# Attention into a bilinear FFN on one core: g turned ahead of the first x, K chunks reordered in the first two units, last half group copied by one engine

## The chip, the cores and the metric

The kernel runs on one core of a Trainium2 chip. The metric is the device time of one launch in microseconds (us). Each time is the median of several runs. "Span" is the time in the profile from the first to the last instruction of the program; it is about 1.8 us shorter than the device time of the same run.

## The reference

Per batch (8) and head (8), with 576 tokens and head width 64: `kv = k^T v`, `out = q kv`, then RMS normalisation over the head width, times `g_norm`. The result, 4608 x 512, goes through `(x @ w_a * x @ w_b) @ w_out` with 512 -> 1536 -> 512.

```python
kv  = np.einsum('bhsd,bhse->bhde', k, v)
out = np.einsum('bhsd,bhde->bhse', q, kv)
rms = np.sqrt(np.mean(out * out, axis=-1, keepdims=True) + 1e-06)
x   = (out / rms * g_norm)            # -> [4608, 512]
y   = (x @ w_a) * (x @ w_b) @ w_out
```

## The kernel before

The FFN goes by strips of 512 tokens, nine of them. A strip has twelve "units" (one per 128 columns of d_ff: four matmuls with w_a, four with w_b, one per K chunk of 128 rows), then four output groups with w_out. Attention of batch b+1 is woven into the FFN of strip b. Attention of batch 0 has nothing to hide behind; it is the prologue. PE is TensorE, which does the matmuls; it writes its results to PSUM, a memory in banks that ScalarE (ACT) and VectorE (DVE) read. All loads of weights and of q, k, v that cast on the way are issued by GpSimd (POOL) into one queue, in a fixed order: pairs of batch 0, w_a and w_b, w_out, pairs of batch 1, then batch 2. A load "lands" when the last of its DMA engines has reported, by the record of the profile.

The prologue (the loop over pairs of heads p; "px" is q kv, "psq" its square on ScalarE, "pss" the sum over the head width by a matmul with a block of ones plus the reciprocal root on ScalarE, "pst" the scaling on VectorE). `dummy(n, i)` issues n matmuls on zeros that nothing reads; they keep PE busy:

```python
    A.kv1(0, SS)
    A.kv1_out(0, SS, nc.vector.tensor_copy)
    A.qtr(1, 3)
    A.qtr_out(1, 3)
    A.px(0, X[0])
    A.psq(0, X[0])
    for p in range(1, NP):
        i = X[p % 2]
        A.kv1(p, 3 - p % 2)
        A.kv1_out(p, 3 - p % 2, nc.vector.tensor_copy)
        A.pss(p - 1, SS)
        if p < NP - 1:
            if p == 1:      # g_norm from a row to a column, by a matmul with 1.0
                nc.tensor.matmul(P[:, 1, 0:1], lhsT=g_row, rhs=one, start=True, stop=True)
                nc.vector.tensor_copy(g_col, P[:, 1, 0:1])
            dummy(1, 2 + p % 2)
            A.qtr(p + 1, 3 - p % 2)
            ...                                    # cut: qtr_out, pst(p - 1)
            A.px(p, i)
            A.psq(p, i)
            dummy(2, 2 + p % 2)
    ...                                            # cut: px(3), its squares by halves, pst(2)
    u0 = Unit(0, 0, 2, 3)                          # first unit: PSUM banks 2, 3
    u1 = Unit(0, 1, 4, 5)
    u0.first((0, 1))                               # K chunks 0 and 1 (w_a, then w_b)
    A.pss(3, SS, (0,)); A.pst(3, X[1], (0,))       # last pair, first half of the tokens
    u0.first((2,))
    A.pss(3, SS, (1,)); A.pst(3, X[1], (1,))       # second half
    u1.first((0, 1, 2))
    u0.rest((3,))                                  # chunk 3 needs both halves of the last pair
    u1.rest((3,))
    for fc in range(2, FC):
        ffn_ab(0, fc)
```

Then batch 1's attention goes between half groups of strip 0's output. Each step does `qtr` and `kv1` of one pair, for which q, k and v of that pair must have landed:

```python
    for n, (g, fcs) in enumerate(pieces):          # six pieces of six matmuls
        o_mm(0, g, O, fcs)
        if fcs is h2:
            o_out(0, g, O)                         # copy and store of a group (stores by the sync engine)
        ...                                        # cut: pss, pst of pair n-2; x, psq of pair n-1
        if n < NP:
            A.qtr(n, 2)
            A.kv1(n, 2)
            ...
```

Batch 2's kv comes in one block in strip 1 after its fifth unit (`k0 = 4`). The end of the kernel, the last half group (256 columns), by halves through two engines:

```python
    o_mm(last, 3, 6, range(FC), hw, d_model)       # PSUM bank 6
    hq = hw + hw // 2
    nc.scalar.copy(o_sb[2][:, hw:hq], P[:, 6, hw:hq])
    store(r0, o_sb[2], hw, hq, nc.scalar)
    nc.vector.tensor_copy(o_sb[3][:, hq:], P[:, 6, hq:])
    store(r0, o_sb[3], hq, d_model)
```

Of the kernel before, what the change touches and what calls it, by code (L numbers as in the profile page):

```python
# [8 lines left out]
FP32 = mybir.dt.float32  # L9
# [6 lines left out]
def kernel(  # L16
# [11 lines left out]
    nc = tc.nc  # L28

    B, H, S, D = q.shape  # L30
    d_model = H * D
# [17 lines left out]
    def sb(shape, dt, name):  # L49
        return pool.tile(shape, dt, name=name, tag=name)  # L50
# [20 lines left out]
    sq = [sb([128, 2, HF], BF16, f"sq{i}") for i in range(3)]  # L71
    rs = [sb([128, 2, HF], FP32, f"rs{i}") for i in range(3)]
    o_sb = [sb([128, d_model], FP32, f"osb{i}") for i in range(4)]
    ident = sb([128, 128], BF16, "ident")
    ones = sb([128, 128], BF16, "ones")
    zeros = sb([128, STRIP], BF16, "zeros")
    g_col = sb([128, 1], FP32, "g_col")
# [5 lines left out]
    g_row = sb([1, 128], FP32, "g_row")  # L83
    one = sb([1, 1], FP32, "one")
    gate = sb([1, 1], BF16, "gate")

    P = psum.tile([128, 8, STRIP], FP32, name="P", tag="P")
# [171 lines left out]
    def store(t0, t, e0, e1, eng=nc.sync):  # L259
        i = 0  # L260
        while i < 128:
            b, j = divmod(t0 + i, S)
            if b < EARLY:
                c, p = divmod(j, EP)
                n = min(128 - i, EP - p)
                r0 = b * S + EC * p + c
                o = out[r0 : r0 + EC * (n - 1) + 1 : EC, e0:e1]
            else:
                n = min(128 - i, S - j)
                o = out[t0 + i : t0 + i + n, e0:e1]  # L270
            eng.dma_start(out=o, in_=t[i : i + n, e0:e1])
            i += n
# [3 lines left out]
    def o_mm(s, g, i, fcs, e0=0, e1=d_model):  # L276
        for fc in fcs:
            nc.tensor.matmul(  # L278
                P[:, i, e0:e1],
                lhsT=abt[s % 2][fc][:, g * 128 : (g + 1) * 128],  # L280
                rhs=wo_t[:, fc, e0:e1],
                start=(fc == 0),
                stop=(fc == FC - 1),
            )
# [16 lines left out]
    def dummy(n, i, cols=STRIP):  # L301
        for _ in range(n):
            nc.tensor.matmul(
                P[:, i, 0:cols], lhsT=zeros[:, 0:128], rhs=zeros[:, 0:cols], start=True, stop=True
            )
# [47 lines left out]
    A.kv1_out(0, SS, nc.vector.tensor_copy)  # L353
    A.qtr(1, 3)
    A.qtr_out(1, 3)
    A.px(0, X[0])
    A.psq(0, X[0])
    for p in range(1, NP):
        i = X[p % 2]
        A.kv1(p, 3 - p % 2)  # L360
        A.kv1_out(p, 3 - p % 2, nc.vector.tensor_copy)
        A.pss(p - 1, SS)
        if p < NP - 1:
            if p == 1:
                nc.tensor.matmul(P[:, 1, 0:1], lhsT=g_row, rhs=one, start=True, stop=True)
                nc.vector.tensor_copy(g_col, P[:, 1, 0:1])
            dummy(1, 2 + p % 2)
            A.qtr(p + 1, 3 - p % 2)
            A.qtr_out(p + 1, 3 - p % 2)
            A.pst(p - 1, X[(p - 1) % 2])  # L370
            A.px(p, i)
            A.psq(p, i)
            dummy(2, 2 + p % 2)
    A.px(3, X[1])
    for h in range(2):
        nc.scalar.activation(sq[0][:, h, :], P[:, X[1] + h, 0:HF], AF.Square)
# [1 line left out]
    u0 = Unit(0, 0, 2, 3)  # L378
    u1 = Unit(0, 1, 4, 5)
    u0.first((0, 1))  # L380
    A.pss(3, SS, (0,))
    A.pst(3, X[1], (0,))
    u0.first((2,))
    A.pss(3, SS, (1,))
    A.pst(3, X[1], (1,))
    u1.first((0, 1, 2))
    u0.rest((3,))
    u1.rest((3,))
    for fc in range(2, FC):
# [23 lines left out]
    u0 = Unit(1, 0, 2, 3)  # L413
    u1 = Unit(1, 1, 4, 5)
# [51 lines left out]
    hw = d_model // 2  # L466
    r0 = last * STRIP + 3 * 128
# [1 line left out]
    nc.vector.tensor_copy(o_sb[3][:, 0:hw], P[:, 5, 0:hw])  # L469
    store(r0, o_sb[3], 0, hw)  # L470
    o_mm(last, 3, 6, range(FC), hw, d_model)
    hq = hw + hw // 2
    nc.scalar.copy(o_sb[2][:, hw:hq], P[:, 6, hw:hq])
    store(r0, o_sb[2], hw, hq, nc.scalar)
    nc.vector.tensor_copy(o_sb[3][:, hq:], P[:, 6, hq:])
    store(r0, o_sb[3], hq, d_model)


# [28 lines left out]
```

## Time and profile before

| | before |
|---|---|
| time, median of 3 runs | 323.25 us (323.0 to 324.08) |
| span of the profiled run | 321.9 us |
| PE busy | 313.7 us (97%) |
| third unit of strip 0 begins (its first weight load) | 18.87 us |
| kv of batch 2 begins | 60.30 us |
| last matmul ends (modelled) | 318.32 us |

The page of the kernel before, its first part: busy time of each engine, share of the span, instructions.

```profile
PE 313.7 (97%) x1912; PEld 151.1 (47%) x1947; DVE 124.0 (39%) x215; ACT 125.3 (39%) x216; POOL 60.3 (19%) x82
```

PE is all but full. What a change can win is in the few places where PE is not working, or works on something that need not be there.

The timeline of the kernel before, PE alone, from the pair loop. Columns: start, duration, engine, source line, operation, tiles, shapes, count; in brackets the idle time of the engine just before, and what ended it.

```profile
9.01 0.41 PE L188 MATMUL P<-sq,ones 128*128 128x288 bf16 x2 [0.20 <-ACT sq L184]
9.35 0.38 PE L365 MATMUL P<-one,g_row 1*128 1x1 f32 x2
9.65 0.39 PE L303 MATMUL P<-zeros 128*128 128x512 bf16 x1
9.97 0.45 PE L161 MATMUL P<-ident,qt 96*64 96x96 bf16 x12
10.35 0.43 PE L175 MATMUL P<-qT,kvs 64*64 64x288 bf16 x4
...
11.56 0.42 PE L188 MATMUL P<-sq,ones 128*128 128x288 bf16 x2
11.82 0.38 PE L303 MATMUL P<-zeros 128*128 128x512 bf16 x1
```

From the sum (L188) to the dummy (L303) it takes 0.64 us where the matmuls of g (L365) stand between, and 0.26 us one pair later. The Trainium skill, "PSUM — Partial Sum Buffer", section "Engine vs sequencer instructions", says that matmuls start and complete in program order, and nothing in these traces stands against it. So g delays the next px (L175) by about 0.38 us.

The same timeline at the end of the prologue, lines of PE and VectorE.

```profile
15.35 0.29 PE L188 MATMUL P<-sq,ones 128*128 128x288 bf16 x1
...
16.10 0.39 PE L234 MATMUL P<-xt,wa_t 128*128 128x512 bf16 x1 [0.47 <-DMA wa_t<-in_moe_w_a_dram]
...
16.57 0.39 PE L234 MATMUL P<-xt,wb_t 128*128 128x512 bf16 x1
...
16.79 0.29 PE L188 MATMUL P<-sq,ones 128*128 128x288 bf16 x1
...
17.65 0.52 DVE L202 SCALAR_TENSOR_TENSOR xt<-P,g_col,rs 128x288 bf16<-128x288 f32 x1 [0.93 <-ACT rs L192]
...
18.22 0.38 PE L234 MATMUL P<-xt,wa_t 128*128 128x512 bf16 x1
```

PE stands until w_a's chunks 2 and 3 land (16.05), then nearly again for w_b's (16.52). The second half's sum (16.79) is queued behind these two matmuls although its data was ready (ScalarE's squares ended at 15.51), and chunk 3 (18.22) waits for what follows from it.

The timeline where kv of batch 2 begins:

```profile
60.30 0.38 PE L137 MATMUL P<-vt,kt 96*64 96x64 bf16 x13 [0.16 <-DMA vt<-in_v_dram]
```

And the tail, the timeline after the last matmul (318.32). The three lines are the copies of the last half group and ScalarE's store.

```profile
318.58 0.27 ACT L473 COPY osb<-P 128x128 f32<-128x128 f32 x1 [4.86 <-DMA out_dram<-osb]
318.88 0.38 ACTq L271 DMA_DIRECT2D out_dram<-osb  x1
318.88 0.29 DVE L475 COPY osb<-P 128x128 f32<-128x128 f32 x1 [1.41 <-ACT osb L473]
```

ScalarE waits for the old store of the tile that it reuses (landed 318.43), and the profile has two semaphore instructions of ScalarE between 318.45 and 318.54, ahead of the copy; VectorE waits for ScalarE. The Trainium skill, "PSUM — Partial Sum Buffer", section "PSUM bank collisions raise a hardware error", says that ScalarE and VectorE may not even read the same partitions of one bank at the same time, and that the compiler's scheduler adds a dependency for this. The trace agrees as far as it goes: VectorE starts 0.03 us after ScalarE ends (318.85), on data that was there 0.56 us before. (The 1.41 us in brackets is all of VectorE's idle time; most of it passed before the data was there.)

### The profile page before, as it was taken

Reading aid. Unit: us, or ns where it says so; the run is one execution under the profiler, and the core shown is the slowest. Engines: PE = TensorE matmul, PEld = TensorE weight load, DVE = VectorE, ACT = ScalarE, POOL = GpSimd, SP = SyncE. Lnnn points to the kernel's source line nnn. Section 1 sums busy time; section 2 is a strip of 40 time slices with the busy share of each in tenths; the row PEclk is TensorE's granted clock in tenths of the full one; section 3 lists DMA queues with packets and bytes.
Section 4 is the critical chain, followed back from the end, with each engine's and each line's share of the span. In section 5 each row is a group of like instructions: output and inputs, shape, how many; then the busy total and the mean of one; then the engine's idle time right before and its main releaser. Section 6 shows DMA issues by size and latency. Waiting matters only on the chain.

```text
span 321.9 us, 4806 instructions
## 1 busy us (share of the span) xinstructions
PE 313.7 (97%) x1912; PEld 151.1 (47%) x1947; DVE 124.0 (39%) x215; ACT 125.3 (39%) x216; POOL 60.3 (19%) x82
## 2 busy tenths in 40 slices
PE   8899999999999999999999999999999999999995
PEld 3444454444444444444444445444544444444443
DVE  3544335344234433453244424532354243313421
ACT  3642255353345433552355325432453233123310
POOL 8854870230041230500050000000000000000000
PEclk9999999999999999999999999999999999999999
DMA  8999999796369899693597150003000200020002
GB/s 177 196 196 199 192 204 216 136 134 117 91 99 160 120 171 220 66 175 80 139 110 113 65 132 9 2 33 99 2 0 2 98 33 0 35 85 14 2 33 98
DMA packets 70043, 32.61 MB, mean 101 GB/s; under 512 B 43652, under 2 KB 65540, under 8 KB 70020
## 3 DMA queue, kind: packets, MB, share of 16 engines
q0 software_dynamic: 49712, 18.44, 48.5%
q1 hardware_dynamic: 19952, 13.50, 15.8%
q10 hardware_dynamic: 356, 0.36, 0.4%
q8 instruction: 15, 0.25, 0.3%
q14 instruction: 8, 0.07, 0.1%
HBM read 37.75 MB, written 12.98 MB: 158 GB/s over the span
## 4 chain that ended last, share of the span: by engine, by line
PE 79%; DMA 14%; POOL 4%; issue 1%; DVE 0%; ACT 0%; POOLq 0%; ACTq 0%
PE P L234 49%; PE P L278 25%; DMA wa_t<-in_moe_w_a_dram 5%; DMA vt<-in_v_dram 4%; DMA wo_t<-in_moe_w_out_dram 2%; PE P L214 2%; PE P L188 2%; DMA qt<-in_q_dram 2%; PE P L137 2%; POOL qs L119 1%; POOL vt L96 1%; POOL kt L96 1%; DMA out_dram<-osb 1%; POOL qt L96 1%; POOL wa_t L331 0%
## 5 line engine op out<-in xcount | busy, mean ns | idle before, releaser
L250 DVE TENSOR_TENSOR ab<-P,asb 128x512 bf16<-128x512 f32 x108 | 74.5, 692 | 124.3 <-PE P L234 123.3
L234 PE MATMUL P<-xt,wa_t 128*128 128x512 bf16 x422 | 111.1, 379 | 1.4 <-DMA wa_t<-in_moe_w_a_dram 0.5
L234 PE MATMUL P<-xt,wb_t 128*128 128x512 bf16 x419 | 110.0, 379 | 0.4
L278 PE MATMUL P<-wo_t,ab 128*128 128x512 bf16 (+1 forms) x433 | 97.3, 373 | 0.6
L248 ACT CAST asb<-P 128x512 bf16<-128x512 f32 x108 | 63.0, 585 | 81.5 <-PE P L234 80.0
L234 PEld LDWEIGHTS <-wb_t 128*128 128x128 bf16 x432 | 42.3, 98 | 51.2 <-DMA wb_t<-in_moe_w_b_dram 0.4
L278 PEld LDWEIGHTS <-ab 128*128 128x128 bf16 x444 | 43.1, 98 | 45.6
L234 PEld LDWEIGHTS <-wa_t 128*128 128x128 bf16 x432 | 41.7, 98 | 45.0 <-DMA wa_t<-in_moe_w_a_dram 0.9
L202 DVE SCALAR_TENSOR_TENSOR xt<-P,g_col,rs 128x288 bf16<-128x288 f32 x64 | 30.2, 513 | 25.1 <-ACT rs L192 25.1
L192 ACT ACTIVATE rs<-P,eps_t 128x576 f32<-128x576 f32 (+1 forms) x33 | 24.0, 726 | 22.2 <-PE P L188 18.2
L291 ACT COPY osb<-P 128x512 f32<-128x512 f32 x17 | 9.9, 585 | 48.6 <-PE P L278 44.9
L184 ACT ACTIVATE sq<-P 128x576 bf16<-128x576 f32 x31 | 20.2, 650 | 20.1 <-PE P L214 18.0
L293 DVE COPY osb<-P 128x512 f32<-128x512 f32 x18 | 12.4, 692 | 32.4 <-PE P L278 32.3
L119 POOL DMA_DIRECT2D qs<-in_q_dram x12 | 19.6, 1634 | 1.7 <-issue 1.7
L116 POOL COPY gate<-qT 1x1 bf16<-1x1 bf16 x5 | 0.9, 176 | 92.2 <-DMA qT<-qs 92.2
L188 PE MATMUL P<-sq,ones 128*128 128x288 bf16 x64 | 13.2, 286 | 0.2 <-ACT sq L184 0.2
L214 PE MATMUL P<-qT,kvb 128*128 128x288 bf16 x56 | 11.7, 286 | 0.0
L148 ACT CAST kvb<-P 64x256 bf16<-64x256 f32 (+1 forms) x20 | 6.0, 301 | 12.0 <-PE P L137 11.9
L137 PEld LDWEIGHTS <-kt 96*64 96x64 bf16 x384 | 7.4, 112 | 4.3 <-issue 3.6
L96 POOL DMA_DIRECT2D vt<-in_v_dram x13 | 9.2, 706 | 1.4 <-DMA qt<-in_q_dram 0.7
L188 PEld LDWEIGHTS <-ones 128*128 128x128 bf16 x64 | 6.1, 98 | 7.0 <-issue 0.2
L96 POOL DMA_DIRECT2D kt<-in_k_dram x13 | 9.3, 712 | 0.0
(42 smaller groups left out, 66.0 us busy)
## 6 DMA issues: line engine op xcount, KB each, us to landing
out_dram<-osb SPq DMA_DIRECT2D x23, 256.0 KB, 2.0
qs<-in_q_dram POOLq DMA_DIRECT2D x12, 288.0 KB, 6.6
kt<-in_k_dram POOLq DMA_DIRECT2D x6, 576.0 KB, 8.6
vt<-in_v_dram POOLq DMA_DIRECT2D x6, 576.0 KB, 11.0
out_dram<-osb SPq DMA_DIRECT2D x13, 128.0 KB, 2.3
wo_t<-in_moe_w_out_dram POOLq DMA_DIRECT2D x12, 128.0 KB, 6.3
wa_t<-in_moe_w_a_dram POOLq DMA_DIRECT2D x5, 256.0 KB, 9.3
wb_t<-in_moe_w_b_dram POOLq DMA_DIRECT2D x5, 256.0 KB, 9.9
```

Source lines behind the costliest of these rows:

```text
L96: nc.gpsimd.dma_start(out=t[:, hs, :, :], in_=src[b, hs].rearrange("h (t c) d -> t h c d", c=EC))
L119: nc.gpsimd.dma_start(out=d[:, hs, :], in_=q[b, hs].rearrange("h t d -> t h d"))
L137: nc.tensor.matmul(o[j * D : (j + 1) * D, :], lhsT=kt[self.b % NB][:, 2 * p + j, c, :], rhs=vt[self.b % NB][:, 2 * p + j, c, :], start=(c ...
L184: nc.scalar.activation(sq[p % 3], P[:, i0 : i0 + 2, 0:HF], AF.Square)
L188: nc.tensor.matmul(P[:, i0 + h, 0:HF], lhsT=ones, rhs=sq[p % 3][:, h, :], start=True, stop=True)
L192: nc.scalar.activation(rs[p % 3][:, h0:h1, :], P[:, i0 + h0 : i0 + h1, 0:HF], AF.Abs_reciprocal_sqrt, bias=eps_t,)
L202: nc.vector.scalar_tensor_tensor(out=xt[p][:, t0 : t0 + HF], in0=P[:, x0 + h, 0:HF], scalar=g_col, in1=rs[p % 3][:, h, :], op0=ALU.mult, o ...
L214: nc.tensor.matmul(P[:, i0 + h, 0:HF], lhsT=kvb[self.b % 2][:, p, :], rhs=self.qT[:, p, h * HF : (h + 1) * HF], start=True, stop=True,)
L234: nc.tensor.matmul(self.a if w is wa_t else self.b, lhsT=w[:, kc, self.fc * 128 : (self.fc + 1) * 128], rhs=xt[kc][:, t0 : t0 + STRIP], st ...
L248: nc.scalar.copy(self.t, self.a)
L250: nc.vector.tensor_mul(abt[self.s % 2][self.fc], self.b, self.t)
L278: nc.tensor.matmul(P[:, i, e0:e1], lhsT=abt[s % 2][fc][:, g * 128 : (g + 1) * 128], rhs=wo_t[:, fc, e0:e1], start=(fc == 0), stop=(fc == F ...
```

## The change

The intent: take the matmul of g out of the chain of the pair loop, and put it where PE idled (before px of the first pair); fill the wait for the weights of chunks 2 and 3 with chunks 0 and 1 of the second unit; and end the kernel with one copy into a fresh tile, which waits for no store and for no other engine.

```diff
+    o_end = sb([128, d_model // 2], FP32, "o_end")
     ...
     A.qtr_out(1, 3)
+    nc.tensor.matmul(P[:, 1, 0:1], lhsT=g_row, rhs=one, start=True, stop=True)
+    nc.vector.tensor_copy(g_col, P[:, 1, 0:1])
     A.px(0, X[0])
     ...
         if p < NP - 1:
-            if p == 1:
-                nc.tensor.matmul(P[:, 1, 0:1], lhsT=g_row, rhs=one, start=True, stop=True)
-                nc.vector.tensor_copy(g_col, P[:, 1, 0:1])
             ...
-            dummy(2, 2 + p % 2)
+            dummy(1 if p == 1 else 2, 2 + p % 2)
     ...
     u0.first((0, 1))
     A.pss(3, SS, (0,))
     A.pst(3, X[1], (0,))
-    u0.first((2,))
+    u1.first((0, 1))
     A.pss(3, SS, (1,))
     A.pst(3, X[1], (1,))
-    u1.first((0, 1, 2))
+    u0.first((2,))
+    u1.first((2,))
     ...
-    hq = hw + hw // 2
-    nc.scalar.copy(o_sb[2][:, hw:hq], P[:, 6, hw:hq])
-    store(r0, o_sb[2], hw, hq, nc.scalar)
-    nc.vector.tensor_copy(o_sb[3][:, hq:], P[:, 6, hq:])
-    store(r0, o_sb[3], hq, d_model)
+    nc.scalar.copy(o_end, P[:, 6, hw:])
+    nc.scalar.dma_start(out=out[r0 : r0 + 128, hw:], in_=o_end)
```

## The prediction

> **What bounds the kernel now.** The page gives PE (matmul) 313.7 of 321.9 us (97%) at full granted clock. The timeline shows what is open: the prologue (0 to 18.2 us), one wait at 60.30 us, and the tail after PE's last matmul (318.3 us).
>
> **Start of the kernel.**
> - g: its matmul sits inside a loop PE -> ScalarE square -> PE sum -> next px. Sum to dummy takes 0.64 us with g (9.01 to 9.65), 0.26 without (11.56 to 11.82): g costs 0.38. Ahead of the first px it takes about 0.2 back (PE idled 0.20 there): px(0) slips from 7.83 to 8.05. Net about 0.15 earlier.
> - One dummy (0.21 us) less: hidden by ScalarE's square (ends 11.47; the sum began 11.56). Worth 0 to 0.05.
> - Chunks: PE stood from 15.64 to 16.10 for wa_t chunks 2-3 (landed 16.05), then for wb_t (16.52), and the second half's sum, queued behind, came at 16.79. After, four matmuls of u1 (0.86 us) fill this hole and the sum starts near 16.3. Its normalisation (DVE, 17.65 to 18.17) ends near 17.7, and chunk 3 starts about 0.45 earlier (18.22 -> 17.75).
> - Head: about 0.45 us. The cap is the next wb_t load (landed 19.19, used 19.73).
>
> **But I expect most of it lost.** Batch 1's vt loads land close before use (45.10 for 45.27; 47.43 for 47.73), and at 60.30 PE waits 0.16 us for batch 2's vt (landed 60.26). POOL issues these loads from a queue that PE does not gate, and DMA is busy nearly throughout (196 GB/s over 20-40 us). PE runs in order, so 0.45 us gained at 20 us is given back as longer waits at 45 to 60.3 us. An earlier transpose DMA (52.87) may compete with that load. After 60.3 PE is busy throughout. Net of the head: 0, from -0.1 (worse) to +0.4.
>
> **End of the kernel.** The chain of waits ends: store of osb2 (landed 318.43), ScalarE copy 318.58 to 318.85, DVE copy 318.88 to 319.17, store issue 319.20, semaphore 320.79. ScalarE waited for the old store of its reused tile, and DVE for ScalarE. The Trainium skill, "PSUM — Partial Sum Buffer", section "PSUM bank collisions raise a hardware error", explains this: accesses of one bank by two engines must be kept apart, reads too; the trace agrees (DVE waited 1.41 us, until ScalarE ended). After: one ScalarE copy of 256 columns from 318.34. From 128 columns at 0.27 and 512 at 0.585 us I estimate 0.37; issue near 318.74. The 64 KB ScalarE store took 1.64 to land; for 128 KB I estimate 1.7, so 320.45: 0.35 to 0.4 earlier, all on the critical path.
>
> **Prediction.** 323.25 - 0.38 (tail) - 0.07 (head) = 322.8 us, range 322.2 to 323.4. Faster by over 2%: 0.01; within 2%: 0.985; slower: 0.005.
>
> **What would show each step.** Right: chunk 3 of u0 near 17.75; PE's wait for vt near 60.3 grown from 0.16 to about 0.5 (or spread over 45 to 60.3); a ScalarE copy of about 0.37 us ending 0.4 us after the last matmul, span near 321.5. Wrong: kv of batch 2 near 59.9, or the last matmul before 318.1: the head's gain survived.
>
> **What would make it wrong.** The vt load landing earlier (then up to 0.4 more, 322.4) or later or varying from run to run (three runs of before spread by 1.1 us); one larger store landing more slowly than two halves.

## The result, and the profile after

| | before | after |
|---|---|---|
| time, median of 6 runs each | 323.41 us (323.0 to 324.79) | 323.21 us (323.05 to 323.52) |
| ratio after / before | | 0.9987, 95% interval 0.9968 to 1.0006 |
| span of the profiled run | 321.9 us | 321.4 us |
| third unit begins | 18.87 us | 18.16 us |
| kv of batch 2 begins | 60.30 us | 60.03 us |
| last matmul ends | 318.32 us | 318.04 us |
| last matmul to the end of the span | 3.59 us | 3.34 us |

A ratio is the mean time of one kernel's runs over that of the other's runs of the same rounds, so it is not quite the ratio of the medians quoted beside it. The verdict is "same" at 2%, and the interval does not exclude no change at all. The sets of runs overlap; what differs most is before's slowest run.

The page of the changed kernel, first part:

```profile
PE 315.2 (98%) x1946; PEld 151.2 (47%) x1946; DVE 123.7 (38%) x214; ACT 125.4 (39%) x216; POOL 60.3 (19%) x82
```

The PE count is not to be compared with before: 34 more records, though the program has one matmul and one weight load fewer. Some records are missing from each trace.

The timeline of the changed kernel, PE alone, in the pair loop:

```profile
7.70 0.38 PE L357 MATMUL P<-one,g_row 1*128 1x1 f32 x2
8.01 0.43 PE L176 MATMUL P<-qT,kvs 64*64 64x288 bf16 x4
...
9.19 0.41 PE L189 MATMUL P<-sq,ones 128*128 128x288 bf16 x2 [0.43 <-ACT sq L185]
9.43 0.38 PE L304 MATMUL P<-zeros 128*128 128x512 bf16 x1
9.74 0.45 PE L162 MATMUL P<-ident,qt 96*64 96x96 bf16 x12
10.12 0.43 PE L176 MATMUL P<-qT,kvs 64*64 64x288 bf16 x4
```

g now costs 0.18 us (px of the first pair at 8.01 instead of 7.83), and its old place is closed: the second px comes at 10.12 instead of 10.35.

The end of the prologue, PE and VectorE:

```profile
15.23 0.59 PE L235 MATMUL P<-xt,wa_t 128*128 128x512 bf16 x2
...
15.66 0.59 PE L235 MATMUL P<-xt,wb_t 128*128 128x512 bf16 x2
...
16.09 0.29 PE L189 MATMUL P<-sq,ones 128*128 128x288 bf16 x1
...
16.95 0.52 DVE L203 SCALAR_TENSOR_TENSOR xt<-P,g_col,rs 128x288 bf16<-128x288 f32 x1 [0.51 <-ACT rs L193]
17.52 0.38 PE L235 MATMUL P<-xt,wa_t 128*128 128x512 bf16 x1 [0.28 <-DVE xt L203]
```

Four matmuls of the second unit fill the hole. Chunk 3 starts at 17.52 instead of 18.22: 0.70 us earlier. Strip 0 keeps this lead through its units: the first transposes of batch 1 start at 39.62 instead of 40.33 us. Then it goes. PE's timeline where batch 1's pairs 2 and 3 begin (L138 is kv), and at kv of batch 2:

```profile
44.89 0.38 PE L138 MATMUL P<-vt,kt 96*64 96x64 bf16 x12 [0.16 <-DMA vt<-in_v_dram]
...
47.66 0.38 PE L138 MATMUL P<-vt,kt 96*64 96x64 bf16 x12
...
60.03 0.95 PE L138 MATMUL P<-vt,kt 96*64 96x64 bf16 x48
```

In the profile before, the first two of these began at 45.27 and 47.73, without a wait; PE's timeline:

```profile
45.27 0.35 PE L137 MATMUL P<-vt,kt 96*64 96x64 bf16 x12
...
47.73 0.35 PE L137 MATMUL P<-vt,kt 96*64 96x64 bf16 x12
```

So the lead is 0.71 us at 39.6, 0.38 at 45, 0.07 at 47.7. The load records say why: v of pair 2 landed at 44.85 and v of pair 3 at 47.62, each 0.04 us before PE went on. The lead of 0.27 us at batch 2's kv is these 0.07 us and another 0.20 that the kernel before lost there, waiting for a v that landed at 60.26; this time it landed at 59.46.

The tail, the timeline after the last matmul (318.04):

```profile
318.08 0.37 ACT L473 COPY o_end<-P 128x256 f32<-128x256 f32 x1 [4.62 <-PE P L279]
318.48 0.38 ACTq L474 DMA_DIRECT2D out_dram<-o_end  x1
```

### The profile page after: what moved, and what is told of

It reads as the page before. It is cut to its first block, busy times and chain, and to the rows that moved or that the text cites. A ratio compares the mean times of both kernels' runs of the same rounds, so it can differ in the third digit from the quotient of the medians.

```text
span 321.4 us, 4834 instructions
## 1 busy us (share of the span) xinstructions
PE 315.2 (98%) x1946; PEld 151.2 (47%) x1946; DVE 123.7 (38%) x214; ACT 125.4 (39%) x216; POOL 60.3 (19%) x82
## 4 chain that ended last, share of the span: by engine, by line
PE 84%; DMA 9%; POOL 4%; issue 1%; ACT 0%; POOLq 0%
PE P L235 52%; PE P L279 27%; DMA wb_t<-in_moe_w_b_dram 6%; DMA vt<-in_v_dram 2%; PE P L189 2%; PE P L215 2%; PE P L138 2%; DMA qt<-in_q_dram 2%; POOL wo_t L112 1%; POOL qt L97 1%; POOL kt L97 1%; POOL vt L97 1%; POOL wa_t L332 0%; POOL wb_t L332 0%; POOL wa_t L108 0%
## 5 line engine op out<-in xcount | busy, mean ns | idle before, releaser
L235 PE MATMUL P<-xt,wb_t 128*128 128x512 bf16 x432 | 111.8, 379 | 0.0
L138 PEld LDWEIGHTS <-kt 96*64 96x64 bf16 x384 | 7.4, 112 | 4.3 <-issue 3.9
```

Source lines behind the costliest of these rows:

```text
L138: nc.tensor.matmul(o[j * D : (j + 1) * D, :], lhsT=kt[self.b % NB][:, 2 * p + j, c, :], rhs=vt[self.b % NB][:, 2 * p + j, c, :], start=(c ...
L235: nc.tensor.matmul(self.a if w is wa_t else self.b, lhsT=w[:, kc, self.fc * 128 : (self.fc + 1) * 128], rhs=xt[kc][:, t0 : t0 + STRIP], st ...
```

## The experiments

Twelve more runs were made, of ten kernels, the changed one and the one before among them again. All gave right results. They ran on three chips; e1, e2, e9 and e10 share one, before_again, after_again, e9_again and e7 the second, the other four the third. Three theories were set against each other. Theory A: the head's gain (0.7 us by the two profiles) is given back at the loads of batches 1 and 2, and what stays is the tail's. Theory B: the head's gain survives and the tail gives nothing. Theory C: something other than the loads takes the gain back.

All profiles together first, because single times can't carry the argument. "F" is when the third unit's first weight load starts. "Given back" is the time from F to kv of batch 2 beyond 41.20 us, the time that this stretch takes when PE waits for nothing in it (and beyond 41.85 us for the two kernels with 0.65 us of added work). "v2" and "v3" are the landings of v of batch 1's pairs 2 and 3, with the start of their kv behind the slash. Columns of times are in us.

| profile | first kv | F | F less first kv | v2 / kv | v3 / kv | kv of batch 2 | given back | kv of batch 2 to last matmul | last matmul to end |
|---|---|---|---|---|---|---|---|---|---|
| before | 7.13 | 18.87 | 11.74 | 45.10 / 45.27 | 47.43 / 47.73 | 60.30 | 0.24 | 258.01 | 3.59 |
| before_again | 7.12 | 18.74 | 11.61 | 45.08 / 45.14 | 48.19 / 48.23 | 60.60 | 0.67 | 258.01 | 3.59 |
| e1_tail_only | 7.13 | 18.51 | 11.38 | 45.04 / 45.08 | 47.81 / 47.85 | 60.22 | 0.51 | 258.01 | 3.37 |
| e5_own_tile | 7.13 | 18.56 | 11.43 | 44.72 / 44.96 | 47.10 / 47.42 | 59.95 | 0.19 | 258.01 | 3.35 |
| e6_chunks_only | 7.71 | 19.02 | 11.32 | 44.36 / 45.42 | 47.14 / 47.88 | 60.23 | 0.00 | 258.01 | 3.59 |
| e10_before_stores_behind | 7.14 | 18.45 | 11.31 | 43.88 / 44.86 | 46.09 / 47.31 | 59.66 | 0.00 | 258.01 | 3.65 |
| after | 7.14 | 18.16 | 11.03 | 44.85 / 44.89 | 47.62 / 47.66 | 60.03 | 0.67 | 258.01 | 3.34 |
| after_again | 7.14 | 18.16 | 11.03 | 44.95 / 45.00 | 47.68 / 47.72 | 60.09 | 0.73 | 258.01 | 3.34 |
| e2_head_only | 7.40 | 18.43 | 11.03 | 45.00 / 45.04 | 47.06 / 47.52 | 59.87 | 0.24 | 258.01 | 3.57 |
| e7_dose3 | 7.12 | 18.93 | 11.80 | 44.10 / 45.98 | 47.54 / 48.43 | 60.78 | 0.00 | 258.01 | 3.37 |
| e12_dose3_again | 7.70 | 18.73 | 11.03 | 44.07 / 45.78 | 47.03 / 48.23 | 60.59 | 0.00 | 258.01 | 3.33 |
| e9_after_stores_behind | 7.69 | 18.72 | 11.03 | 43.96 / 45.12 | 46.17 / 47.57 | 59.92 | 0.00 | 258.01 | 3.33 |
| e9_again | 7.13 | 18.16 | 11.02 | 44.33 / 44.65 | 46.54 / 47.10 | 59.45 | 0.10 | 258.50 | 3.35 |
| e11_stores_behind_x_later | 6.89 | 18.98 | 12.10 | 44.31 / 45.38 | 46.53 / 47.84 | 60.19 | 0.01 | 258.12 | 3.36 |

### The tail alone: e1_tail_only

The kernel before with the diff's lines of `o_end` and of the last five statements, and nothing else.

> The kernel before with only the new tail (last half group copied by ScalarE to its own tile). Theory A (the head's gain is given back at the loads of batches 1 and 2, so the whole gain is the tail's): span 0.2 to 0.4 us under before, time ratio 0.9988 +- 0.0008, like the full change; prologue marks as before (chunk 3 of the first unit at 18.2, kv of batch 2 at 60.3); ScalarE copy 0.37 us, starts 0.03 after the last matmul. Theory B (the head's gain survives to the end and the tail gives nothing): ratio 1.000, span as before.

Measured: 323.5 us, median of 6 (before 323.55 of 11), ratio 1.0002, interval 0.9983 to 1.002. In time this misses the expectation, and with that interval it refutes nothing either: one of its runs took 324.73 us. The profile has the expected tail: 3.37 us from the last matmul to the end, 0.22 less than before. Span 321.6, 0.3 under before's first profile, of which 0.09 is an earlier last matmul.

### The head alone: e2_head_only

The changed kernel with the old last five statements.

> The changed kernel with the old tail. Theory A: time within 0.2 us of before (ratio 0.9995 +- 0.0008) although chunk 3 of the first unit starts near 17.5 instead of 18.2 and strip 0's last units run 0.7 us earlier; PE waits again at the vt loads of batch 1 (45 and 47.6) and kv of batch 2 starts between 60.0 and 60.3. Theory B: kv of batch 2 near 59.6, last matmul near 317.6, ratio 0.998.

Measured: 323.4 us, median of 5, ratio 0.9992 (0.9977 to 1.0006). kv of batch 2 at 59.87 us, a little earlier than expected, and not at 59.6 as theory B would have it. The prologue began 0.26 us late in this run (first kv at 7.40), so PE came to batch 1's loads 0.26 us later than in "after"; it gave back 0.24 us instead of 0.67.

### Strip 0's stores behind the loads: e9_after_stores_behind and e10_before_stores_behind

The first has the edit on the changed kernel, the second on the kernel before:

```diff
-        store(s * STRIP + g * 128, t, 0, d_model)
+        store(s * STRIP + g * 128, t, 0, d_model, nc.gpsimd if s == 0 else nc.sync)
```

GpSimd has issued all loads of batches 1 and 2 by then, and its queue takes the stores behind them. The Trainium skill, "DMA: Bandwidth & Descriptors", section "Issuing engines are not separate DMA queues", says that DMAs from different engines run on the same 16 DMA engines and interleave. So strip 0's 1 MB of stores, issued by the sync engine from 39 us on, should slow the loads. The table agrees: from v of pair 1 to v of pair 3 takes 5.15 to 5.84 us in the ten profiles with the stores on the sync engine, and 4.41 to 4.45 us in the four with the stores behind.

> The changed kernel; the output stores of strip 0 (1 MB, in the DMA engines from 39 to 57 us) are issued by POOL behind the loads of batches 1 and 2, so those loads get the DMA engines to themselves. Theory A (loads of batches 1 and 2 swallow the head's 0.7 us): the last vt of batch 1 lands under 47.0, vt of batch 2 under 58; no PE wait at 45, 47.6 or 60; kv of batch 2 near 59.4 to 59.6 and the last matmul near 317.5: 0.5 to 0.6 us under the changed kernel, ratio to before 0.997. Theory C (something other than these loads takes the gain back, such as a slower PE pace): loads land early and the marks at 60 and 318 stay where they are, ratio 0.9987.

> The kernel before with the same shift of strip 0's stores. Theory A: only the 0.16 us wait at 60.3 goes, so 0.1 to 0.2 us under before (ratio 0.9995), and 0.9 to 1.0 us over the changed kernel with shifted stores: the head's 0.7 plus the tail's 0.3, both in full. If the shift helps both kernels alike, theory A falls.

Measured: the changed kernel with the shift 322.84 us (median of 6), ratio 0.998 (0.9964 to 0.9995); the kernel before with the shift 323.28 us (median of 5), ratio 0.9988 (0.9974 to 1.0002).

PE waited nowhere between F and kv of batch 2 in either, and the loads landed about as early as expected. But theory A as I had written it did not come out whole. Counted from the first kv matmul to the last matmul, to take out the start of the run, the shift gave the changed kernel 310.90 - 310.24 = 0.66 us, and the kernel before 311.19 - 310.53 = 0.66 us (single profiles; the next section has a second set): alike, where I had expected 0.5 to 0.6 and 0.1 to 0.2. By my own words theory A falls in this form. What was wrong with it is in the table. The old head does not always take 11.74 us to F; in four other profiles with both the old order and the old place of g it takes 11.31 to 11.61. And the old kernel, too, gives back at the loads, 0.19 to 0.67 us. With the loads out of the way the two kernels are 0.29 us apart at the last matmul (310.53 and 310.24), which is the difference of their heads in these runs (11.31 and 11.03). So in this pair the head's gain did survive when the loads let it, but it is 0.3 us where the weights land early, not 0.7. One thing helped: the profile of e9 began 0.55 us late (first kv at 7.69), so its loads had that much more time; e10 began on time. The next section has e9 with a start on time.

### The two kernels again: before_again, after_again, e9_again

No edit.

> The kernel before, unchanged, for a second profile. Wanted: how much its prologue varies. The first profile of before started the third unit 11.74 us after the first kv matmul; the runs with the old chunk order that followed gave 11.31 and 11.38. If the old order hangs on when the weights land, this comes out between 11.2 and 11.8; from the third unit to the kv of batch 2 it takes 41.2 us plus the waits for vt. From kv of batch 2 to PE's last matmul: 258.0 us, as in all profiles so far.

> The changed kernel, unchanged, a second profile and more times. With the new chunk order the third unit starts 11.02 us after the first kv matmul (11.02 to 11.03 in three profiles so far). Theory A: PE again arrives early at batch 1's vt of pairs 2 and 3 and gives back 0.2 to 0.7 us there; 258.0 us from kv of batch 2 to the end. Ratio to before 0.998 to 1.000.

> The changed kernel with strip 0's stores behind the loads, unchanged, for a second profile and more times. Theory A: no PE wait between the third unit and kv of batch 2 (41.2 us), so faster than the changed kernel of the same rounds by 0.3 to 0.6 us; ratio to before 0.9970 to 0.9985.

Measured: before_again took 11.61 us to F and then waited at pair 3's v, PE's timeline:

```profile
48.23 0.26 PE L137 MATMUL P<-vt,kt 96*64 96x64 bf16 x5 [0.46 <-DMA vt<-in_v_dram]
```

after_again: 323.25 us (median of 5) against 323.34 of before (9 runs), ratio 0.9993 (0.9981 to 1.0006); 11.03 us to F, 0.73 given back. e9_again: 323.0 us (5), ratio 0.9989 (0.9976 to 1.0003); 0.1 us faster than the changed kernel in the means of the same rounds, where I had expected 0.3 to 0.6. Its profile shows where a part went, PE's timeline:

```profile
64.30 0.28 PE L215 MATMUL P<-qT,kvb 128*128 128x288 bf16 x1 [0.33 <-DMA qT<-qs]
```

The first x of batch 2 now waits for the transpose of batch 2's q, which landed at 64.25: 258.50 us from kv of batch 2 to the last matmul, 0.49 more than in nearly all others. Moving the DMA work turned one wait into another one in this run. That the delayed stores held up the transpose is argued and not shown: in e10, with the same stores behind, it landed at 61.58.

This profile began on time (first kv at 7.13), and so it is the fairer partner of e10. PE still gave back 0.10 us, at v of batch 1's pairs 0 and 1 (landed 39.89 and 42.13, each 0.04 us before its kv), and none at pairs 2 and 3. At kv of batch 2 it was 0.21 us ahead of e10 (59.45 and 59.66): most of the head's 0.3 us. After the wait for the transpose nothing was left; counted from the first kv, its last matmul ended at 310.83, behind e10's 310.53.

### Added work: e7_dose3 and e12_dose3_again

```diff
     for fc in range(2, FC):
+        if fc == 6:
+            dummy(3, 7)
         ffn_ab(0, fc)
```

> The changed kernel with three zero matmuls of 512 columns (0.65 us of PE work that nothing needs) between units 5 and 6 of strip 0, after the prologue and ahead of batch 1's attention. Theory A: PE would have waited about that long at batch 1's vt, so the added work disappears: no PE wait at 45 and 47.6, kv of batch 2 at 60.0 to 60.3 as without it, span within 0.3 us of the changed kernel's. Theory B (no slack there): everything after it 0.65 us later, kv of batch 2 near 60.7, span near 322.0.

Measured: 323.96 us (one run), kv of batch 2 at 60.78. Inconclusive: a w_b load of the prologue landed at 15.38 instead of about 14.1 us, and the third unit came 0.77 us late for that. PE's timeline of this run:

```profile
15.43 0.39 PE L235 MATMUL P<-xt,wb_t 128*128 128x512 bf16 x1 [0.65 <-DMA wb_t<-in_moe_w_b_dram]
```

> The same three added zero matmuls (0.65 us), run again because in the first run of it a wb load of the prologue landed at 15.38 instead of about 14.1 us and PE came 0.77 us late for that reason alone. Theory A: with the prologue as in the changed kernel (third unit at 18.2 to 18.4), kv of batch 2 starts at 60.0 to 60.4 in spite of the added 0.65 us, PE waits little or nothing at 45 and 47.6, and the ratio to before is 0.9990 to 1.0005. Theory B: kv of batch 2 at 60.7 or later, ratio 1.0010 to 1.0020.

Measured: 323.45 us (median of 5), ratio 1.0001 (0.9986 to 1.0016); kv of batch 2 at 60.59. The profiled run had no lead to lose: its prologue started 0.57 us late (first kv at 7.70, see the last section), PE reached batch 1's loads after they had landed, and the added 0.65 us came on top in full. So the profile agrees with neither theory as I had put it. It does agree with the account of the table, in which PE goes on at the later of its own arrival and the landing. The time is 0.20 to 0.24 us over the changed kernel's medians of other rounds, 323.25 and 323.21. An added 0.65 us that some runs hide and some don't would give such a number, but these rounds don't show that it is so.

### The tail by its parts: e5_own_tile

The kernel before; only ScalarE's quarter goes to a tile of its own.

```diff
-    nc.scalar.copy(o_sb[2][:, hw:hq], P[:, 6, hw:hq])
-    store(r0, o_sb[2], hw, hq, nc.scalar)
+    nc.scalar.copy(o_end[:, 0 : hw // 2], P[:, 6, hw:hq])
+    nc.scalar.dma_start(out=out[r0 : r0 + 128, hw:hq], in_=o_end[:, 0 : hw // 2])
```

> The kernel before; only ScalarE's quarter of the last half group goes to a tile of its own, still half the columns by each of two engines. If the old tail lost its time to the store of the reused tile (ScalarE began 0.26 us after the data was there) this saves about 0.22 us: from PE's last matmul to the end of the span 3.37 us instead of 3.59, nearly as much as the changed kernel's 3.34. DVE must still start after ScalarE's copy ends (one bank of PSUM). If one copy by one engine is what saves, the tail stays near 3.55.

Measured: 3.35 us from the last matmul (317.96) to the end, as expected. The timeline of this run's tail:

```profile
318.00 0.27 ACT L474 COPY o_end<-P 128x128 f32<-128x128 f32 x1 [4.62 <-PE P L279]
318.29 0.38 ACTq L475 DMA_DIRECT2D out_dram<-o_end  x1
318.29 0.29 DVE L476 COPY osb<-P 128x128 f32<-128x128 f32 x1 [1.18 <-ACT o_end L474]
```

The fresh tile is what saves: ScalarE begins 0.04 us after the last matmul instead of 0.27. VectorE still starts only when ScalarE has ended. To use one engine instead of two added nothing that this can see (3.35 against 3.34): the copy is done 0.21 us sooner (0.44 instead of 0.65 us from the last matmul to the issue of the last store), but one store of 128 KB took 1.76 us from issue to the end of the wait for it where the last of two with 64 KB took 1.60, and the waits at the end of the program took 0.04 us longer.

### The order of chunks alone: e6_chunks_only

The kernel before with the diff's five changed lines around `u0.first` and `u1.first`.

> The kernel before with only the order of chunks changed (g and the dummies as before). My account: from the first kv matmul to the third unit 11.3 us (11.02 with the whole change, 11.31 to 11.74 before), because g and the dummy give 0.28 and the order gives the rest; and no PE wait for chunks 2 and 3 of the weights. If the order gives nothing when the weights are early, 11.3 is also what before takes in its best profile, so this part is worth 0 to 0.4 us according to when the weights land.

Measured: 11.32 us to F, and no wait for the weights of chunks 2 and 3, in a run whose prologue began late. The whole change takes 11.03, so g and the dummy are worth 0.29 us. The old order and the old g took 11.31 to 11.74 us in five profiles, with PE waiting 0.30 to 0.47 us at chunk 2 in each, until 15.93 to 16.10. By the profiles that wait ended with w_a in before and before_again (landed 16.05 and 15.92). In e1, e5 and e10 w_a landed at 15.80 to 15.88, and the profiles name VectorE's x of pair 2, done at about 15.9, as what came last.

What ranks the five is the next load, w_b's chunks 2 and 3. It landed at 16.07, 16.16, 16.21, 16.39 and 16.52 us where the stretch to F took 11.31, 11.38, 11.43, 11.61 and 11.74, and F came 2.35 us after it in the last four (2.38 in the first). With w_b early the new order gains nothing: the second half's sum starts 9.24 us after the first kv in e6 as in e10. So against these five the order of chunks was worth 0 to 0.4 us, according to when w_b landed.

### A version meant to beat both: e11_stores_behind_x_later

e9 with batch 2's first x one unit later:

```diff
         k0, kn, xs = (4, 1, (6, 9, 11, 13)) if s < 3 else (2, 1, (4, 7, 10, 12))
+        if s == 1:
+            xs = (7, 9, 11, 13)
```

> The changed kernel with strip 0's stores behind the loads, and batch 2's first x one unit later, so that it does not wait for the transpose (0.33 us wait at 64.3 in the second profile of the shifted stores). Theory A: no PE wait from the third unit to the end: last matmul 310.2 us after the first kv matmul (310.9 changed kernel), ratio to before 0.9970 to 0.9985, the fastest of all.

Measured: 323.01 us (median of 6; before 323.46 of 11), ratio 0.9984 (0.9967 to 1.0002). Three of its six runs took 322.63 to 322.71 us; before's best of eleven took 323.01. The profiled run was not one of those: a w_b load landed at 15.43 us, PE stood 0.94 us in the prologue, and the marks that I had named (310.2 us from the first kv to the last matmul) came out at 311.4. The wait for the transpose did not appear. Over the three timings of kernels with shifted stores and the new head the ratios are 0.998, 0.9989 and 0.9984; only the first interval excludes 1. Their medians are 322.84, 323.0 and 323.01 us, against 323.21 and 323.25 for the changed kernel and 323.34 to 323.55 for before in the experiments' rounds. So this looks like the better version, by 0.2 to 0.4 us over the changed kernel and 0.3 to 0.7 over before by these medians, at the edge of what these rounds can show.

## Why the prediction was right or wrong

The time was right: 323.21 us lies in 322.2 to 323.4, and the forecast change, 0.45 us, is close to the measured 0.42 (ratio 0.9987) and 0.23 (0.9993, second set). Neither set excludes zero. That the sum fits so well is in part luck. It was forecast as 0.38 for the tail and 0.07 for the head; the two profiles show 0.25 for the tail, and 0.28 for the head at the last matmul (318.04 instead of 318.32). An oversized tail and an undersized head cancel. The prediction had also named a sign of being wrong, "the last matmul before 318.1: the head's gain survived", and by it the head was wrong in this profile: 0.28 of its 0.70 us survived. (The second profile of the changed kernel has 318.11.) Point by point:

- **PE bounds the kernel; after 60.3 us it is busy throughout: right.** From kv of batch 2 to the last matmul it took 258.01 us in twelve of fourteen profiles, with both kernels.
- **g: right in kind, a little undersized.** It cost 0.18 us in its new place (0.2 predicted) and gave 0.41 in its old one: 0.23 net at the second px, where 0.15 was predicted. The dummy gave 0.05 more.
- **The order of chunks: right in mechanism, mis-sized against this one profile.** Chunk 3 started 0.70 us earlier, not 0.45; 0.42 of it is the order. The sum of the second half started at 16.09, not 16.3. What the prediction had not seen is that this term has no fixed size: the old order takes 11.31 to 11.74 us to the third unit, as w_b's chunks 2 and 3 land. The profile that I costed it from was the worst of five for the old order. The new order with g moved took 11.02 or 11.03 us in six of eight profiles; in the other two a late load of the first chunks stopped it.
- **Most of the head's gain is lost at the loads: right, and shown for these profiles; what is left was put too low (0.07, measured 0.28).** "PE's wait for vt near 60.3 grown from 0.16 to about 0.5 (or spread over 45 to 60.3)": it was spread, 0.33 us at pair 2 and 0.32 at pair 3, none at 60.03. With the loads relieved, PE waited nowhere in this stretch in e9 and e10, and their difference in the head (0.28 us) arrived at the last matmul (0.29), with e9's late start to help; in e9_again, which started on time, 0.21 us of it arrived at kv of batch 2. What the prediction missed is that the kernel before runs into the same loads: it gave back 0.19 to 0.67 us there. So the old head's bad luck is hidden there as well as the new head's gain, and the difference of the two kernels behind the loads is smaller than either.
- **"Batch 2's vt" as the last wall: half right.** It held PE in the profile before and for 0.19 us in e5_own_tile; in before_again, e1_tail_only and both profiles of the changed kernel pair 3 of batch 1 was what held it last, in e2_head_only pair 2. That v of batch 2 landed 0.80 us earlier in the profile after (59.46 against 60.26) is why 0.27 us of the lead was left at kv of batch 2.
- **The tail: right in mechanism, oversized.** Predicted 0.35 to 0.4, measured 0.25 (3.59 to 3.34). The prediction's own end points give 0.34 (320.79 to 320.45), and it used 0.38. The term that was mis-sized is the landing of the larger store: the copies gave 0.44 us, about as predicted (last matmul to issue 0.88 -> 0.44), the store took 0.15 us more (1.61 -> 1.76 to the end of the wait, where 0.11 was predicted, 1.59 -> 1.7), and 0.04 us went to the waits at the end of the program, which the prediction had left out. The Trainium skill, "DMA: Bandwidth & Descriptors", section "Anatomy of one DMA — SWDGE (gpsimd) path", fits a DMA with a constant plus bytes over 436 GB/s; an estimate from its second term for 64 KB more is 0.15 us. These stores were not issued by GpSimd, and the traces agree only in part: from the sync engine's 64 KB to ScalarE's 128 KB the landing took 0.15 us more (1.59 to 1.74), but between ScalarE's own two sizes only 0.10 (1.64 to 1.74).

What stays open: how much of the head's gain an average run keeps. The last matmul ended at 317.96 to 318.61 us in the four profiles with the old head and the stores unmoved (before, before_again, e1, e5) and at 317.88 to 318.11 in the three with the new (after, after_again, e2). The means are 0.27 us apart, but the ranges overlap; and the times (0.2 to 0.4 us for the whole change, of which the tail is 0.25) can't split it further. Nor is it known what made a w_b load land 1.3 us late in two of fourteen profiles.

## What to carry to other kernels

A gain made early in a kernel with one in-order engine is worth nothing until it has passed the next wait for something that the gain does not speed; here a fixed queue of loads, some 25 us later, took 0.70 us of lead down to 0.28. Before costing a wait from one profile, take a second and a third: this one's size hung on when one load landed. Check the parts of a forecast as well as its sum, since errors can cancel. And a last copy should have a tile of its own: here 0.22 to 0.25 us for one small tile.

## What the Trainium skill lacked or had wrong

- "TensorE: Matmul & The Clock Gate", section "Part 1: The HAM clock gate", gives the time at which PE changes to full speed as varying by ±500 ns from run to run. In the fourteen profiles the first matmul starts at 1.19 or 1.20 us of the span, and the trace's record of the granted clock begins at 3.90 to 6.90 us, a range of 3.0 us; the dummies start 0.43 us apart before that point and 0.22 after it. That fits the free-running window of 3.4 us that the same section names, not ±500 ns. Where it came at 6.86 us or later, the first kv started 0.57 us late (7.69 to 7.71 instead of 7.12 to 7.14). The timelines show it in the dummies: five of them take 2.34 us in e12_dose3_again and 1.48 in the changed kernel. PE alone, first e12_dose3_again:

```profile
3.73 2.34 PE L304 MATMUL P<-zeros 128*128 128x512 bf16 x5
```

  and the changed kernel:

```profile
3.73 1.48 PE L304 MATMUL P<-zeros 128*128 128x512 bf16 x5
```

- The same section says that the ramp is under 1% of a typical span and need not be fitted. That holds here (its jitter is 0.57 us of 322), but the jitter is larger than the change's 0.2 to 0.4 us: for a study of 0.1% it has to be taken out, by counting from a mark after it.
- "DMA: Bandwidth & Descriptors" gives the constant of about 2.0 us for the path through GpSimd; for a store issued by ScalarE or the sync engine on trn2 this page has no time from issue to landing. Here the last stores took 1.58 to 1.65 us (64 KB) and 1.73 to 1.76 us (128 KB) from issue to landing.
- The same page's section "Issuing engines are not separate DMA queues" says that DMAs of different engines interleave, without a size. Here, with strip 0's stores among the loads, the last six loads of batch 1 (from v of pair 1 to v of pair 3) took 0.7 to 1.4 us longer: 5.15 to 5.84 us, against 4.4 without. In the profile before, 0.5 MB of the 1 MB had been issued when the last of these loads landed.
